# Masking the second batch's scores by bfloat16 factors on TensorE in a fused attention and Fourier-mixing kernel

## The chip, the cores and the metric

The kernel runs on one core of a Trainium2 chip. The metric is the time of one execution on the device in microseconds, of the slowest core; here there is only one core. Times are medians over several runs. A profile is one execution recorded by the hardware profiler, with its own time.

The engines are named as in the profile: PE is TensorE (matmuls; its weight loads are PEld), DVE is VectorE, ACT is ScalarE, POOL is GpSimd, and SP is SyncE, which here only issues DMAs. Every engine executes its own instructions in the order in which the program issued them.

## The reference

Four batches, eight heads, 768 positions, head dimension 64. Block-sparse attention with a mask of 32 x 32 blocks is followed by a Fourier mixing layer with two channel matmuls:

```python
scores = scale * np.matmul(q, k.transpose(0, 1, 3, 2))
# mask: neighbouring, first, last and sampled blocks; it is the same for all batches and heads
scores = np.where(mask, scores, -1000000000.0)
scores = scores - np.max(scores, axis=-1, keepdims=True)
attn = np.exp(scores)
attn = attn / (np.sum(attn, axis=-1, keepdims=True) + 1e-09)
x = np.matmul(attn, v)                      # then (B, H, S, D) -> (B, S, H*D)

X = np.fft.fft(np.fft.fft(x, axis=1), axis=2)
u = x + np.real(X)
un = (u - mean(u)) / np.sqrt(var(u) + 1e-06)
out = u + np.maximum(un @ w_ch1, 0.0) @ w_ch2
```

The mask depends on block rows and block columns alone, so the additive form of it is a product of two thin factors: one has a row per key block, the other says for every query which blocks are off.

## The kernel before

**Pairs, units and slots.** Heads are taken in pairs, and `n` counts the 16 pairs, four to a batch (`NP` = 4). The scores of a pair are computed with keys on the partitions: `half` chooses 384 of the 768 queries (`HS`), `c` chooses 128 of the keys, and one such piece for both heads is a unit `u`, twelve to a pair (`UP`). Two units make a slot (`SLOT`), so a pair has six slots, a batch has 24 (`SB`), and attention has 96. Batch 0 is slots 0 to 23, batch 1 is slots 24 to 47, and batch 2 begins at slot 48.

**One slot.** `slot(sl)` first issues `scores` for its two units: four logical matmuls (L551) into PSUM tiles `s`, of which there are two, one per unit. Then `weigh` makes the weights `e` of each unit (four buffers). Then `values` multiplies the `e` of the slot before with v into `o` (L597). After that come loads, transposes of the next pair's q and k (`turn`, L486), placing of results in x (`place`, L619), and steps of the mixer.

**How batch 0 is masked.** For `n < NP` the scores of both units are followed by two more matmuls a unit (L559). They add the product of the bfloat16 factors `of_k` and `off_q` to the same PSUM accumulation, so that masked scores become hugely negative. The exponential on ScalarE (L569) then writes `e` directly. The factors lie in two buffers with the tag `acc`. The sums over keys of this batch are made on TensorE (`add_up`, L663).

**How the later batches are masked.** For `n >= NP` the exponential is taken in place in PSUM (L572), and VectorE multiplies it with a table of zeros and ones in bytes into `e` (L574). GpSimd adds the `e` of a half up in `acc` (L584, two adds a unit from the second unit on), in the same two `acc` buffers that held the factors. `total` (L677) sums that over the partitions once a pair.

**The mixer and the channels.** When a batch's attention is done, `begin` appends its mixer's steps to the queue `apart`: division by the sums, folds on VectorE, cosine and sine matmuls (`along`, `across`), adding to x (`arrive`), normalisation (`spread`, `whiten`), transposes (`un_flip`, L917) and combinations for a Strassen-like product (`right`, `left`). The last entry of that queue has the kind "-"; it moves the list `rest` into `late`. `late` holds the channel matmuls (`quad`, L992, and `channels`, L1048), which are 155.6 us of planned TensorE time for a batch.

**What sets the order.** The order of the whole program is fixed when it is built. A planner keeps a modelled clock of each engine in `when`; `busy(engine, us, after)` advances one. `gap` takes steps from `apart` as long as the modelled clocks allow it: a VectorE step (kind "d" or "w") is taken when VectorE's clock would stay within a lead over TensorE's (3.0 us while no channels are waiting, 2.2 otherwise), and a TensorE step when its bank and the step before it are ready. Planned costs are written beside the steps: 0.72 us for the scores of a unit, 0.25 for its two mask matmuls, 0.75 for its values, 0.8 for its exponential, 0.97 for its mask multiplication, 2.0 for its two adds on GpSimd.

**When channels run.** Once channels wait in `late`, a slot takes between 2.5 and 9.6 us of them, so that about 100 us (`COVER`) are left for the start of the next batch. In slot 53 `until` runs whatever is left in `apart` and `late` until the first half of batch 0 is stored, because x has two buffers per half.

**Buffers and queues that the change touches.** `room(i, ...)` gives one of six large buffers. During batch 0 they hold raw weights: `w_load` brings chunk i to buffer i % 6, and `w_round` rounds it on ScalarE and VectorE; there are 32 chunks. The mixer uses buffers 0 and 1 for its folds, 4 and 5 for combinations, and the channels use 2 and 3 for hidden values. All the DMAs of this stretch but the first few are issued by SP, in the order of the program; in slot 21 these are the q loads of pair 5 (`load_q`, L252), which wait until pair 4's q has been read.

Of the kernel before, what the change touches and what calls it, by code (L numbers as in the profile page):

```python
# [12 lines left out]
BF16 = mybir.dt.bfloat16  # L13
# [4 lines left out]
ALU = mybir.AluOpType  # L18
ACT = mybir.ActivationFunctionType
# [83 lines left out]
def kernel(  # L103
# [14 lines left out]
    nc = tc.nc  # L118

    B, H, S, D = q.shape  # L120
    DM = H * D
    FF = w_ch1.shape[1]
    P = 128
    C = S // P
# [3 lines left out]
    HS = S // 2  # L128
# [7 lines left out]
    scale = 1.0 / float(D) ** 0.5  # L136
    KA = D + NB
    NP = H // 2
# [27 lines left out]
    mask = const.tile([P, C, S], U8, name="mask")  # L166
# [25 lines left out]
    def busy(engine, us, after=0.0):  # L192
        when[engine] = max(when[engine], after) + us
        return when[engine]
# [11 lines left out]
    HOP = 0.1  # L206
# [94 lines left out]
    def warm(n):  # L301

        m = ps_m.tile([P, P], FP32, tag="m", name="warm")
        for _ in range(n):
# [5 lines left out]
                         func=ACT.Exp)  # L310
# [124 lines left out]
    def room(i, shape, name, dtype=FP32):  # L435
        return big.tile(shape, dtype, tag=f"big{i}", name=name)
# [29 lines left out]

    turned, e_of, acc_of, o_of, sums_of, x_of, sp_of = {}, {}, {}, {}, {}, {}, {}
    s_at, e_at, oT_at, acc_at = {}, {}, {}, {}  # L470

# [64 lines left out]
    def scores(us):  # L536

        n, w = divmod(us[0], UP)
        half = w // C
        qT, kT = turned[n, 0], turned[n, 1]  # L540
        queries = slice(half * HS, (half + 1) * HS)
        got = []
        for u in us:
            c = u % C
            s = ps_s.tile([P, 2, 512], FP32, tag="s", name="s")
            got.append((u, s))
            busy("PE", 0.72, max(e_at.get(u - SLOT, 0.0), z_at[u % 2]))
            s_at[u] = when["PE"] + HOP
            for i in range(2):
                rows = slice(D * i, D * i + D)  # L550
                nc.tensor.matmul(s[:, i, 0:HS], kT[rows, c * P:(c + 1) * P], qT[rows, queries],  # L551
                                 start=True, stop=n >= NP)
        for u, s in got if n < NP else ():
            c = u % C
            busy("PE", 0.25)
            s_at[u] = when["PE"] + HOP
            for i in range(2):
                rows = slice(D * i, D * i + D)
                nc.tensor.matmul(s[:, i, 0:HS], of_k[rows, c * P:(c + 1) * P], off_q[rows, queries],  # L559
                                 start=False, stop=True)  # L560
        return got

    def weigh(u, s):
        n, w = divmod(u, UP)
        half, c = divmod(w, C)
        e = ep.tile([P, 2, HS], FP32, tag="e", name="e")
        e_of[u] = e
        if n < NP:
            nc.scalar.activation(out=e, in_=s[:, :, 0:HS], func=ACT.Exp, scale=scale)  # L569
            e_at[u] = busy("ACT", 0.8, s_at[u]) + HOP  # L570
            return
        nc.scalar.activation(out=s[:, :, 0:HS], in_=s[:, :, 0:HS], func=ACT.Exp, scale=scale)  # L572
        m = mask[:, c, half * HS:(half + 1) * HS].rearrange("p (o s) -> p o s", o=1)
        nc.vector.tensor_tensor(out=e, in0=s[:, :, 0:HS], in1=m.broadcast_to([P, 2, HS]),  # L574
                                op=ALU.mult)
        e_at[u] = busy("DVE", 0.97, busy("ACT", 0.8, s_at[u]) + HOP) + HOP
        if c > 0:
            acc_at[n, half] = busy("POOL", 2.0, e_at[u]) + HOP
        if c == 1:
            acc_of[n, half] = acc_p.tile([P, 2, HS], FP32, tag="acc", name="acc")  # L580

        for i in range(2 if c > 0 else 0):
            acc = acc_of[n, half][:, i, :]
            nc.gpsimd.tensor_add(out=acc, in0=e_of[u - 1][:, i, :] if c == 1 else acc,  # L584
                                 in1=e[:, i, :])
# [665 lines left out]
    def begin(b):  # L1251


        before, after, rest = mixer(b, x_of[b, 0], x_of[b, 1])
        any_of = len(late) + len(apart) + 4 * len(rest)
        hold = 2 * T
        apart.extend((*step, any_of) for step in norm_steps(b) + before)
        apart.extend((*step, hold) for step in after)
        apart.append(("-", lambda: late.extend(rest), 0.0, 0.0, 0.0, hold))

    def w_loads():
        while state["got"] < min(len(wchunks), state["w"] + ROOMS):
# [3 lines left out]
    def w_steps(sl):  # L1266
        while state["w"] < min(len(wchunks), W_PACE * sl):
            w_round(state["w"])
            state["w"] += 1

    def slot(sl):
        phase, r = divmod(sl, SB)
        n, s = divmod(sl, SP)
        units = range(SLOT * sl, SLOT * sl + SLOT)
        if sl < B * SB:
            for u, ps in scores(units):
                weigh(u, ps)
        if not late:
            gap(1.5)
        if 0 < sl <= B * SB:  # L1280
            done = [u - SLOT for u in units]
            for u in done:
                values(u)
            if phase == 0 or sl == SB:
                add_up(done)
            for u in done:
                e_of.pop(u)
        if s == 3 and n + 2 < len(pairs):
            load_q(n + 2)
        if s == 0 and 0 < n < len(pairs) - 1:  # L1290
            load_k(n + 1)

        reuse = n % NP == 0 and phase >= 2
        if sl > 0 and s == (5 if reuse else 3) and sl <= B * SB:
            b, j = pairs[n]
            at = oT_at[n, 0]
            if reuse:
                until(lambda: (b - 2, 0) in finished)
                at = when["PE"] + LEAVES
            if in_blocks(n):  # L1300
                place_blocks(n, 0)
            else:
                short.append(("t", at, lambda: place(n, 0)))
        if 0 < sl <= B * SB and s == 0 and n % NP != 1:
            if in_blocks(n - 1):
                place_blocks(n - 1, 1)
            else:
                short.append(("t", oT_at[n - 1, 1], lambda: place(n - 1, 1)))
        if sl < B * SB and n % NP == 1 and s == 1:
            b = pairs[n - 1][0]  # L1310
            at = oT_at[n - 1, 1]
            if b >= 2:
                until(lambda: (b - 2, 1) in finished)
                at = when["PE"] + LEAVES
            short.append(("t", at, lambda: place(n - 1, 1)))
        if sl > SB and s == 0 and sl <= B * SB:
            short.append(("t", acc_at[n - 1, 1], lambda: total(n - 1)))
        if n + 1 < len(pairs):
            for at, a, half in ((1, 0, 0), (2 if n > 0 else 3, 0, 1), (4, 1, 0), (5, 1, 1)):
                if s == at and n + 1 < BY_VECTOR:  # L1320
                    short.append(("t", 0.0, lambda a=a, half=half: turn(n + 1, a, half)))
            if s == 1:
                load_v(n + 1)
        if sl == 0:
            short.append(("t", 0.0, lambda: turn(0, 1, 1)))
        if sl == 1:
            short.append(("t", 0.0, lambda: turn(0, 0, 1)))
        if phase == 0 and 4 <= sl < 4 + 2 * C:
            short.append(("m", 0.0, lambda: mask_step(sl - 4)))
        if r == 1 and 0 < phase:  # L1330
            begin(phase - 1)
        left = SB * (phase + (0 if r == 0 else 1)) + 1 - sl
        us = sum(step[1] for step in late)
        pace = max(LEAST, min(MOST, (us - COVER) / left)) if left > 0 else MOST
        state["owed"] = min(state["owed"], pace) + pace if late else 0.0
        gap(max(state["owed"], 0.0))
        while late and state["owed"] >= late[0][1] / 2:
            state["owed"] -= late[0][1]
            channel_step()
            gap(max(state["owed"], 0.0))  # L1340

        while short and (s in (2, 5) or len(short) > 1 or phase == 0 or r == 0):
            ready = [i for i in short if max(i[1], min(free[i[0]])) <= when["PE"] + 0.1]
            if not ready and s not in (2, 5) and r > 0 and sl > 1:
                break
            item = ready[0] if ready else short[0]
            short.remove(item)
            item[2]()
        if BY_VECTOR <= n + 1 < len(pairs):
            for at, fn, args in ((0, squares, (n + 1, 0)), (1, flip_blocks, (n + 1, 0)),  # L1350
                                 (2, in_order, (n + 1,)), (4, flip_blocks, (n + 1, 1)),
                                 (5, squares, (n + 1, 1))):
                if s == at:
                    fn(*args)
        w_loads()
        w_steps(sl)
        if sl >= 4 and sl % 2 == 0:
            table_step()

# [139 lines left out]
```

## Time and profile before

| What | us |
|---|---|
| median of 9 runs | 1094.52 (1091.46 to 1095.35) |
| the profiled execution | 1093.16 |
| its span, first to last instruction | 1091.2 |
| busy in the span: PE | 1050.7 (96%) |
| DVE | 675.2 (62%) |
| ACT | 379.2 (35%) |
| POOL | 270.1 (25%) |
| mask multiplications L574, 144 of them | 131.1, 948 ns each |
| adds L584 on POOL, 192 and 48 | 196.7 and 49.6 |
| mask matmuls L559 of batch 0, 96 of them | 11.8 |

The page gives, for each group of instructions, its line, engine and operation, its tiles, how many there are, the busy time and the mean of one; behind a bar stands how long the engine was idle before them and what ended that. The mean of one contains overlap with its neighbours: a matmul of L559 lasts 323 ns by itself, but the 96 of them keep TensorE busy for 11.8 us.

The span in 40 equal slices of 27.3 us shows where the engines are full. A digit is the busy share in tenths, PEclk the clock that TensorE was granted:

```profile
PE   8999988988999999999999999999999999999996
DVE  5899878498754525564567535555556355575663
POOL 1000277688000001255546000244540001000000
PEclk9999999999999999999999999999999999999999
```

Slices 5 to 10 are batch 1 and the first slots of batch 2: TensorE is not full there, while VectorE and GpSimd are at their densest. From slice 11 on TensorE is full up to the last slice.

### The profile page before, as it was taken

Reading aid. Unit: us, or ns where it says so; the run is one execution under the profiler, and the core shown is the slowest. Engines: PE = TensorE matmul, PEld = TensorE weight load, DVE = VectorE, ACT = ScalarE, POOL = GpSimd, SP = SyncE. Lnnn points to the kernel's source line nnn. Section 1 sums busy time; section 2 is a strip of 40 time slices with the busy share of each in tenths; the row PEclk is TensorE's granted clock in tenths of the full one; section 3 lists DMA queues with packets and bytes.
Section 4 is the critical chain, followed back from the end, with each engine's and each line's share of the span. In section 5 each row is a group of like instructions: output and inputs, shape, how many; then the busy total and the mean of one; then the engine's idle time right before and its main releaser. Section 6 shows DMA issues by size and latency. Waiting matters only on the chain.

```text
span 1091.2 us, 12419 instructions
## 1 busy us (share of the span) xinstructions
PE 1050.7 (96%) x4334; PEld 535.6 (49%) x4334; DVE 675.2 (62%) x1241; ACT 379.2 (35%) x762; POOL 270.1 (25%) x302
## 2 busy tenths in 40 slices
PE   8999988988999999999999999999999999999996
PEld 4433333533555545443444545443344555568575
DVE  5899878498754525564567535555556355575663
ACT  5988655555111102353342202334230302220210
POOL 1000277688000001255546000244540001000000
PEclk9999999999999999999999999999999999999999
DMA  7757211021000000222211000221000001000001
GB/s 222 226 166 239 80 44 44 16 52 36 0 1 1 0 1 26 61 38 44 55 22 34 0 1 10 55 44 39 13 8 8 1 1 29 30 1 1 1 17 45
DMA packets 108194, 46.66 MB, mean 43 GB/s; under 512 B 95822, under 2 KB 100956, under 8 KB 108124
## 3 DMA queue, kind: packets, MB, share of 16 engines
q1 hardware_dynamic: 106236, 44.99, 16.3%
q10 hardware_dynamic: 1856, 0.79, 0.3%
q8 instruction: 36, 0.59, 0.2%
q14 instruction: 34, 0.28, 0.1%
q0 software_dynamic: 32, 0.01, 0.0%
HBM read 37.11 MB, written 6.29 MB: 40 GB/s over the span
## 4 chain that ended last, share of the span: by engine, by line
PE 83%; DVE 9%; ACT 2%; issue 2%; DMA 1%; POOL 1%; DVEq 0%; ACTq 0%; POOLq 0%
PE y L1048 23%; PE z L992 15%; PE s L551 10%; PE o L597 8%; PE yp L992 7%; PE yy L1111 6%; PE xp L992 3%; DVE e L574 3%; PE zp L805 2%; PE zp L776 1%; PE sp L663 1%; DMA out_dram<-x 1%; PE tp L486 1%; DVE x L855 1%; POOL acc L584 1%
## 5 line engine op out<-in xcount | busy, mean ns | idle before, releaser
L584 POOL TENSOR_TENSOR acc<-acc,e 128x384 f32<-128x384 f32 x192 | 196.7, 1058 | 84.3 <-DVE e L574 83.7
L551 PE MATMUL s<-qT,kT 64*128 64x384 f32 x768 | 158.0, 524 | 13.5 <-DVE e L574 11.8
L574 DVE TENSOR_TENSOR e<-s,mask 128x768 f32<-128x768 f32 x144 | 131.1, 948 | 58.9 <-ACT s L572 54.2
L572 ACT ACTIVATE s<-s 128x768 f32<-128x768 f32 x144 | 109.7, 791 | 112.8 <-PE s L551 111.7
L597 PE MATMUL o<-e,vr 128*64 128x384 f32 x768 | 146.7, 503 | 0.0
L1051 DVE TENSOR_TENSOR x<-y,x 128x512 f32<-128x512 f32 x72 | 49.7, 690 | 139.7 <-PE y L1048 139.6
L1048 PE MATMUL y<-w_sb,hA 128*128 128x512 f32 x288 | 129.8, 597 | 1.1 <-ACT zs L807 1.1
L1048 PE MATMUL y<-w_sb,hB 128*128 128x512 f32 x288 | 128.7, 597 | 1.0 <-DVE x L1051 1.0
L551 PEld LDWEIGHTS s<-qT,kT 64*128 64x128 f32 x768 | 63.8, 187 | 89.5 <-DVE e L574 41.9
L584 POOL TENSOR_TENSOR acc<-e 128x384 f32<-128x384 f32 x48 | 49.6, 1054 | 221.1 <-DVE e L574 171.8
L997 DVE TENSOR_TENSOR hA<-z,hA 128x384 f32<-128x384 f32 x64 | 35.7, 557 | 96.3 <-PE z L992 96.3
L992 PE MATMUL z<-unT,t 128*128 128x384 f32 x256 | 93.0, 486 | 0.0
L868 POOL TENSOR_SCALAR st<-st 128x1 f32<-128x1 f32 x24 | 6.6, 276 | 346.9 <-DVE st L867 346.5
L1048 PEld LDWEIGHTS y<-w_sb,hB 128*128 128x128 f32 x288 | 53.3, 190 | 68.5 <-issue 66.5
L597 PEld LDWEIGHTS o<-e,vr 128*64 128x64 f32 x768 | 47.0, 137 | 77.2 <-issue 71.7
L1048 PEld LDWEIGHTS y<-w_sb,hA 128*128 128x128 f32 x288 | 52.9, 190 | 64.8 <-issue 58.3
L1001 ACT ACTIVATE hA<-hA 128x384 f32<-128x384 f32 x64 | 33.4, 523 | 120.1 <-DVE hA L997 119.9
L992 PEld LDWEIGHTS z<-unT,t 128*128 128x128 f32 x256 | 48.6, 190 | 33.9
L1001 ACT ACTIVATE hB<-hB 128x384 f32<-128x384 f32 x64 | 33.5, 523 | 86.3 <-DVE hB L997 86.3
L992 PE MATMUL xp<-unT,w_sb 128*128 128x384 f32 x128 | 48.9, 505 | 1.3 <-DVE x L1051 0.7
L1012 ACT COPY hA<-xp 128x384 f32<-128x384 f32 x32 | 15.3, 478 | 100.0 <-PE xp L992 100.0
L992 PE MATMUL yp<-unT,w_sb 128*128 128x384 f32 x128 | 46.9, 489 | 0.4 <-DVE un L841 0.4
(200 smaller groups left out, 1390.0 us busy)
## 6 DMA issues: line engine op xcount, KB each, us to landing
wraw<-in_moe_w_ch_dram SPq DMA_DIRECT2D x32, 512.0 KB
vr<-in_v_dram SPq DMA_DIRECT2D x30, 192.0 KB
qr<-in_q_dram SPq DMA_DIRECT2D x48, 64.0 KB
x<-oT SPq DMA_DIRECT2D x192, 12.0 KB
kr<-in_k_dram SPq DMA_DIRECT2D x14, 192.0 KB
qb<-in_q_dram SPq DMA_DIRECT2D x28, 96.0 KB
kb<-in_k_dram SPq DMA_DIRECT2D x28, 96.0 KB
out_dram<-x SPq DMA_DIRECT2D x16, 128.0 KB
```

The source lines that it names most:

```text
L551: nc.tensor.matmul(s[:, i, 0:HS], kT[rows, c * P:(c + 1) * P], qT[rows, queries], start=True, stop=n >= NP)
L572: nc.scalar.activation(out=s[:, :, 0:HS], in_=s[:, :, 0:HS], func=ACT.Exp, scale=scale)
L574: nc.vector.tensor_tensor(out=e, in0=s[:, :, 0:HS], in1=m.broadcast_to([P, 2, HS]), op=ALU.mult)
L584: nc.gpsimd.tensor_add(out=acc, in0=e_of[u - 1][:, i, :] if c == 1 else acc, in1=e[:, i, :])
L597: nc.tensor.matmul(o[D * i:D * i + D, :], vt[:, i, c, :], e[:, i, :], start=(c == 0), stop=(c == C - 1))
L805: nc.tensor.matmul(ps[:, 0:KS - 1], sd[:, t, parts[g - 2]], sn_sb[:, t, :], start=(t == 0), stop=(t == T - 1))
L992: nc.tensor.matmul(to, a[:, k, :], c[:, k, :], start=(k == 0), stop=(k == ND // 2 - 1))
L997: tt(out=to, in0=ps, in1=a, op=ALU.add)
L1001: nc.scalar.activation(out=h, in_=h, func=ACT.Relu)
L1048: nc.tensor.matmul(y, hs[0, half][:, l, m * P:(m + 1) * P], w2_sb[:, 4 * r + l, :], start=(l == 0), stop=(l == 3))
L1051: nc.vector.tensor_tensor(out=x[:, m, :], in0=y, in1=x[:, m, :], op=ALU.add)
L1111: nc.tensor.matmul(ps, a[:, k, :], c[k // 2][:, k % 2, :] if isinstance(c, list) else c[:, k, :], start=(k == 0), stop=(k == 3))
```

## The change

In the slots after slot 21, until the step "-" of the first mixer is taken, the scores are masked as in batch 0: behind the score matmuls of both units come the bfloat16 mask matmuls, and the exponential writes `e` directly. From that step on, VectorE multiplies as before. The choice is made for each unit when `scores` is called, and the set `by_pe` remembers it for `weigh`. The condition does not name the batch: it asks whether the factors are still there.

Because the adds of batch 1 need the two `acc` buffers, the factors are copied at the end of slot 21 (`SB - 3`) into large buffer 2 by two DMAs on SP, 128 partitions of 1536 bytes each. From then on the mask matmuls read the copy, in slots 22 and 23 of batch 0 too. The step "-" sets `factors["at"]` to None beside moving the channels to `late`. The planner's costs follow: 0.25 us on TensorE for a unit masked there, and no 0.97 us on VectorE. GpSimd's adds and the sums of the batches are as before.

```diff
+    by_pe = set()
+    factors = {"at": (of_k, off_q)}
+
+    def keep_factors():
+
+        kept = room(2, [P, 2, S], "factors", BF16)
+        for a, t in enumerate(factors["at"]):
+            nc.sync.dma_start(out=kept[:, a, :], in_=t)
+        factors["at"] = kept[:, 0, :], kept[:, 1, :]
...
             got.append((u, s))
+            if n < NP or (factors["at"] and True):
+                by_pe.add(u)
...
-                                 start=True, stop=n >= NP)
-        for u, s in got if n < NP else ():
-            c = u % C
+                                 start=True, stop=u not in by_pe)
+        for u, s in got:
+            if u not in by_pe:
+                continue
+            c, (at_k, at_q) = u % C, factors["at"]
             busy("PE", 0.25)
...
-                nc.tensor.matmul(s[:, i, 0:HS], of_k[rows, c * P:(c + 1) * P], off_q[rows, queries],
+                nc.tensor.matmul(s[:, i, 0:HS], at_k[rows, c * P:(c + 1) * P], at_q[rows, queries],
                                  start=False, stop=True)
...
-        if n < NP:
+        if u in by_pe:
             nc.scalar.activation(out=e, in_=s[:, :, 0:HS], func=ACT.Exp, scale=scale)
             e_at[u] = busy("ACT", 0.8, s_at[u]) + HOP
+        else:
+            nc.scalar.activation(out=s[:, :, 0:HS], in_=s[:, :, 0:HS], func=ACT.Exp, scale=scale)
+            m = mask[:, c, half * HS:(half + 1) * HS].rearrange("p (o s) -> p o s", o=1)
+            nc.vector.tensor_tensor(out=e, in0=s[:, :, 0:HS], in1=m.broadcast_to([P, 2, HS]),
+                                    op=ALU.mult)
+            e_at[u] = busy("DVE", 0.97, busy("ACT", 0.8, s_at[u]) + HOP) + HOP
+        if n < NP:
             return
-        nc.scalar.activation(out=s[:, :, 0:HS], in_=s[:, :, 0:HS], func=ACT.Exp, scale=scale)
...
-        apart.append(("-", lambda: late.extend(rest), 0.0, 0.0, 0.0, hold))
+
+        def go():
+            late.extend(rest)
+            factors["at"] = None
+        apart.append(("-", go, 0.0, 0.0, 0.0, hold))
...
         w_steps(sl)
+        if sl == SB - 3:
+            keep_factors()
```

More of the change, by code (lines that the diff above doesn't have):

```diff
@@ L567, in weigh @@
         e_of[u] = e
-        if n < NP:
+        if u in by_pe:
             nc.scalar.activation(out=e, in_=s[:, :, 0:HS], func=ACT.Exp, scale=scale)
             e_at[u] = busy("ACT", 0.8, s_at[u]) + HOP
-            return
-        nc.scalar.activation(out=s[:, :, 0:HS], in_=s[:, :, 0:HS], func=ACT.Exp, scale=scale)
[L573 to L576, printed above, removed]
+        else:
[5 more added lines that the diff above has]
+        if n < NP:
+            return
         if c > 0:
```

## The prediction

> **What bounds the kernel now.** I read four views in this order: the busy table by stretch, the list of waits of TensorE in the second batch, the order in time around its first slot and around the DMA queue that the change uses, and the occupation of GpSimd.
>
> The busy table (columns: stretch, length, then busy time of PE, PEld, DVE, ACT, POOL, the granted clock, DMA share):
> ```profile
> 0.00:127.50 127.50, 121.64 (x802) 52.23 (x802) 106.64 (x251) 104.32 (x215) 3.68 (x14) 1.00 0.66 196
> 127.50:271.50 144.00, 126.47 (x672) 55.30 (x672) 109.17 (x150) 78.54 (x164) 108.70 (x111) 0.96 0.17 40
> 271.50:292.20 20.70, 20.09 (x61) 11.56 (x61) 16.28 (x31) 5.11 (x10) 2.75 (x2) 0.93 0.00 1
> 292.20:1091.20 799.00, 782.49 (x2804) 416.55 (x2802) 443.07 (x811) 191.27 (x374) 155.01 (x176) 1.00 0.09 20
> ```
> TensorE sets the time: 782 of the last 799 us are busy, and of the 16.5 us missing there about nine are the last stretch's output. The one place with slack is 127.5 to 271.5, the second batch and the first slots of the third: 17.5 us idle, and a clock below 1.
>
> Who ends that idle time, and how:
> ```profile
> PE s L551 <- DVE e L574: 9.8, 8, 2.5
> PE utp L917 <- DVE un L880: 3.1, 1, 3.1
> PE tp L486 <- ACT qT L495: 2.2, 2, 1.1
> ```
> ```profile
> 126.96 0.55 PE L619 MATMUL xt<-ident,oT 128*128 128x128 f32 x3
> 129.78 2.22 PE L551 MATMUL s<-qT,kT 64*128 64x384 f32 x8 [2.27 <-DVE e L574]
> ```
> The scores of a unit need one of two pairs of banks, which the mask multiplication on VectorE releases; VectorE is in order and has weight rounding or the mixer's folds ahead of it. After the stall matmuls run slower: the eight L597 from 131.92 took 2.72 us, against 1.51 elsewhere.
>
> I priced the loss by full-speed spacing. Scores start 1.49 us before their values (150.21 to 151.70), values take 1.44 (to 153.15): 2.93 us a slot. From 127.43 to 271.45 TensorE has 29 slots (85.0), 16 groups of k and x transposes at 0.47-0.48 (7.6), four q turns at 0.95 (3.8), four sums of 0.78, the mixer's along and across steps (9.15 and 4.8), six flips (3.5), two inversions (0.9): 117.9 of 144.0, so 26.1 lost. The two quads that follow end at 292.16 and lose 2.3 more. **Lost: 28.4 us**, by place 4 around 128, 5 up to 150, 6.6 from 150 to 185, 5.6 to 244, 1.9 to 266, 5.7 to 292.
>
> **What the skill says.** (1) "TensorE: Matmul & The Clock Gate", part 1: the clock halves after an idle window of about 3.4 us. The trace agrees in kind, though stalls of 2.3 and 2.5 us already brought it. (2) "SBUF — State Buffer", "Who interferes with whom": a VectorE operation with two SBUF inputs and a GpSimd one that reads SBUF exclude each other for a whole instruction; one with a single SBUF input doesn't contend outside the two-port modes. The trace fits: next to adds, a two-element copy (L740) took 0.96 us, and the similar L857 at 242.10 took 0.15. The mask multiplication has one SBUF input, so its removal frees no port, but it takes away VectorE time in which GpSimd ran undisturbed. (3) "DMA: Bandwidth & Descriptors", "Anatomy of one DMA": about 2.0 us fixed plus bytes over 436 GB/s, fitted on GpSimd's queue. The one landing that this trace has, 13.5 KB on that queue, took 3.0 us; for SP's queue no run here shows it.
>
> **The change, part by part.**
>
> *Copy of the factors.* Two DMAs of 128 x 1536 B at the end of slot 21 go behind q's load on SP:
> ```profile
> 109.45 0.38 SPq L440 DMA_DIRECT2D wraw<-in_moe_w_ch_dram  x1
> 110.67 3.82 SPq L252 DMA_DIRECT2D qr<-in_q_dram  x6
> ```
> SP is free at 114.49. The buffer is free: its last rounded chunk, the 27th, ends at 110.75. Behind both SP has nothing until 124.69, so they delay no load. Landing, an estimate by (3): 114.5 + 0.4 for the second issue + 2.0 + 0.39 MB / 436 GB/s (0.9) = 117.8. But slot 22 already reads the copy: its mask matmuls stand at 115.13. TensorE is in order, so values, x and k transposes of the slot wait too: 2.7 us (1.5 to 6), with the slower clock behind it 1.3 (0 to 2). New loss: 4.
>
> *The masks.* In batch 0 a slot's scores to its values take 1.82 us (109.21 to 111.03) with four bfloat16 matmuls; without, 1.49. So 0.33 us per slot of two units is added. It lasts until the planner takes the step that starts the channels; there is no test for the batch, so it lasts into the third if that comes late. In the kernel before, the start came only at 271, forced in slot 53. The chain of steps up to it has planned costs of 40.9 us VectorE, 18.7 TensorE, 8.4 ScalarE, one after the other, some 68; each of its 18 TensorE steps also waits for the next gap, of which there are two a slot, about 1.2 us: 90. A planned slot costs 3.44 us (0.72+0.25+0.75 twice) and some 0.6 of transposes; with masks no longer on VectorE, nothing else holds the chain. 4.05 N + 18.7 = 90 to 98 gives N = 18 to 20; I take slots 24 to 43, **20 slots: 6.6 us added** (16 to 30 slots: 5.3 to 9.9).
>
> *What leaves.* 40 multiplications of 0.948 us on VectorE, 38 us: on the path only through the waits above. The exponential writes e itself, 0.82 for 0.79 us on ScalarE, which has room (78.5 of 144).
>
> *What is late next.* Around 128, the 4 us before disappear and the 4 of the copy take their place: no gain. To 150: clock and waits on e go, the waits of a q turn on ScalarE (1.1 each) stay: 2.5 of 5. From 150 to 185 the folds run while GpSimd is already full: 4.84, 5.00, 5.00 and 4.84 of 5 us in
> ```profile
> 160.00:165.00 5.00, 4.83 (x5) 1.00 0.04 14
> 165.00:170.00 5.00, 5.00 (x5) 1.00 0.02 5
> 170.00:175.00 5.00, 5.00 (x5) 1.00 0.35 79
> 175.00:180.00 5.00, 4.84 (x5) 1.00 0.00 0
> ```
> Its 20 adds per pair of heads need 20 us alone (1.00 each), and TensorE's pair then takes 6 x 3.26 + 3.6 = 23.2. Folds and scalings ask some 12 us of the same port within seven slots; 23 adds more make 35 against TensorE's 29. Four e tiles allow about one slot of lag, so ScalarE, then TensorE, wait for the rest: 3.5 of 6.6 remain. From the along steps to slot 43: flips behind slow VectorE steps, 3 of 5.6. The later slots have channels to fill waits, 1.5 of 1.9; the start of the channels is no longer forced at one place, 0.5 of 5.7. Sum of the new losses 4 + 2.5 + 3.5 + 3 + 1.5 + 0.5 = 15.
>
> *Moved.* Some 55 us of channels go from one block behind slot 53 into slots 43 to 48 (the pace is capped at 9.6 per slot). TensorE's work is the same wherever it stands; there the masks are on VectorE again, 1.9 + 5.6 us a slot against 13 of TensorE. Slot 53 still forces batch 0 to its end in both kernels, and 88 us remain as cover for the next mixer, whose first steps took 280 to 366. So nothing after it changes.
>
> **Sum.** 28.8 by places (28.4 by count) lost before, 15 after, 6.6 added: 7.2 us less. The profiled execution took 1093.16 (span 1091.2 and 1.96 around it): 1086.0. It stands 1.36 below the median of the runs, so 1087.3.
>
> **Rivals.**
> *A, the forecast*: 1083 to 1092, chance 0.46.
> *B, the waits go almost entirely*: the port holds nobody and the copy lands early; losses 8, result 1080. For it: batch 0 with the same matmuls has PE busy 121.6 of 127.5, first loads included. Against: the queue order above. 0.16.
> *C, the channels start no sooner*: 30 slots cost 9.9, the forced 5.7 stays, a loss of about 19: 28.8 - 19 - 9.9 = 0: 1094.5. For it: real VectorE steps are longer than planned (folds and scalings 20.8 against 15). Against: the planner goes by its own costs. 0.1.
> *D, slower: GpSimd's adds become the bound.* Without masks VectorE sends two-input operations back to back, and each add waits for one. From slot 24 to 36 there are 40 adds and 51 us of TensorE; at 1.15 to 1.25 us, as contended adds took, they fit. From 1.45 they need 58, 7 us over, which cancels the gain; at 1.55, 62, 11 over: 1098. For it: the four rows above. Against: the folds end, and adds beside along steps are free. A copy landing 5 us later would do the same. 0.28.
>
> The chances of faster, same and slower count 0.2% (2.2 us), about what a measurement of this kernel can tell from no change: faster 0.61 (A, B less 0.01), same 0.11, slower 0.28. The likeliest case alone has 1083 to 1092; with B and the near part of D the range is 1079 to 1098.
>
> **What would show it.** A wait of TensorE on a DMA of the copy in slot 22 near 115 us, 2 to 4 us long; none on VectorE's e from slot 24; four bfloat16 matmuls a slot until around slot 43, and the first product of a quad well before the third batch. D shows as ScalarE's exponential waiting for GpSimd, and adds above 1.4 us. The forecast is wrong if the copy costs over 6 us or if idle time between slots 24 and 43 stays above 15.

## The result, and the profile after

| | before | changed |
|---|---|---|
| median of the runs, us | 1093.82 (1091.46 to 1095.35, 30 runs) | 1087.94 (1084.66 to 1090.86, 10 runs) |
| ratio, 95% interval | 1 | 0.9949 (0.9939 to 0.9959) |
| span of the profiled execution, us | 1091.2 | 1086.1 |

The kernel is faster by 5.9 us in the medians and by 5.1 us in the profiles. Single runs of the changed kernel lie up to 6.2 us apart, so its profile shows one of several possible courses. The channels now start at 227 us, in slot 42, instead of at 271 in slot 53. So TensorE masks 19 slots of batch 1, slots 24 to 42. Line numbers have moved: scores are L565, mask matmuls L575, values L615, mask multiplications L590, GpSimd's adds L602, the first cosine step L794 to L796.

First, who ended idle time of TensorE in the second batch of the changed kernel, over 107 to 300 us (columns: total us, times, longest). Tiles of the program stand in front: `s` is scores, `zp` a cosine step, `tp` a transpose, and `sa` and the `e` of L767 are folds:

```profile
PE s L575 <- DMA factors<-at_q: 3.8, 1, 3.8
PE zp L794 <- DVE sa L767: 3.7, 1, 3.7
PE tp L498 <- ACT qT L507: 2.2, 2, 1.1
PE zp L795 <- DVE e L767: 0.7, 1, 0.7
PE s L565 <- ACT e L585: 0.3, 1, 0.3
```

The waits on VectorE's e, 9.8 us before, are gone, and so is the forced flip at 270. Two waits are new: on the copy of the factors, and on VectorE's folds.

Second, the busy table by stretch, for the changed kernel (columns as before). The first three rows run from the scores of slot 22 to 330 us; the next runs on to the scores of slot 58, from where both kernels issue the same work; the last is the rest:

```profile
113.21:160.00 46.79, 38.24 (x231) 16.36 (x232) 37.16 (x57) 25.88 (x50) 25.11 (x19) 0.96 0.19 49
160.00:227.00 67.00, 65.17 (x403) 32.49 (x401) 32.74 (x61) 38.05 (x84) 47.15 (x54) 1.00 0.14 36
227.00:330.00 103.00, 102.69 (x390) 48.02 (x387) 57.83 (x87) 35.78 (x71) 36.84 (x36) 1.00 0.10 20
330.00:462.15 132.15, 129.68 (x441) 67.05 (x439) 75.78 (x148) 31.62 (x67) 22.09 (x27) 1.00 0.08 19
462.15:1086.10 623.95, 608.62 (x2241) 326.42 (x2241) 351.40 (x631) 154.19 (x295) 139.28 (x154) 0.99 0.10 21
```

The same two parts of the kernel before, from slot 22 to slot 58 and the rest:

```profile
113.68:469.41 355.73, 336.25 (x1383) 162.87 (x1384) 230.54 (x388) 132.16 (x272) 126.49 (x134) 0.98 0.11 25
469.41:1091.20 621.79, 606.61 (x2243) 326.09 (x2241) 351.21 (x631) 154.07 (x295) 139.97 (x155) 1.00 0.10 21
```

From slot 22 to slot 58 the changed kernel takes 348.94 us instead of 355.73: 6.8 less. Its four rows have 13.2 us of idle TensorE, against 19.5. TensorE's busy time is nearly equal although 6.3 us of mask matmuls came in: time at the slow clock and score groups split by a wait (1.78 us instead of 1.56) went out, together some 7 us, an estimate from the durations of the matmuls in both traces. VectorE is busy for 27 us less. Two thirds of the idle time that is left, 8.6 us of 13.2, lie in the first row, which is also the only one of the four with a granted clock below 1. The last part then gives 2.2 us back, although it does the same work.

### The profile page after: what moved, and what is told of

Same layout as the page of the kernel before. It is cut to its first block, busy times and chain, and to the rows that moved or that the text cites. A ratio compares the mean times of both kernels' runs of the same rounds, so it can differ in the third digit from the quotient of the medians.

```text
span 1086.1 us, 12509 instructions
## 1 busy us (share of the span) xinstructions
PE 1051.8 (97%) x4410; PEld 536.7 (49%) x4410; DVE 648.3 (60%) x1203; ACT 378.6 (35%) x762; POOL 274.2 (25%) x302
## 4 chain that ended last, share of the span: by engine, by line
PE 89%; DVE 5%; ACT 2%; DMA 2%; issue 1%; SPq 1%; DVEq 0%; ACTq 0%
PE y L1066 23%; PE z L1010 15%; PE s L565 11%; PE o L615 11%; PE yp L1010 8%; PE yy L1129 6%; PE xp L1010 4%; PE zp L823 2%; PE sp L681 1%; PE tp L498 1%; PE utp L935 1%; PE s L575 1%; PE sp L695 1%; PE zp L794 1%; PE xt L637 1%
## 5 line engine op out<-in xcount | busy, mean ns | idle before, releaser
L602 POOL TENSOR_TENSOR acc<-acc,e 128x384 f32<-128x384 f32 x192 | 200.4, 1077 | 128.5 <-DVE e L590 119.1
L565 PE MATMUL s<-qT,kT 64*128 64x384 f32 x768 | 154.2, 517 | 5.2 <-DVE e L590 3.8
L615 PE MATMUL o<-e,vr 128*64 128x384 f32 x768 | 147.0, 504 | 0.0
L590 DVE TENSOR_TENSOR e<-s,mask 128x768 f32<-128x768 f32 x106 | 96.3, 948 | 46.8 <-ACT s L588 45.1
L588 ACT ACTIVATE s<-s 128x768 f32<-128x768 f32 x106 | 80.2, 789 | 118.3 <-PE s L565 112.7
L602 POOL TENSOR_TENSOR acc<-e 128x384 f32<-128x384 f32 x48 | 49.9, 1060 | 233.8 <-ACT e L585 128.4
L565 PEld LDWEIGHTS s<-qT,kT 64*128 64x128 f32 x768 | 63.7, 186 | 80.1 <-issue 23.0
L615 PEld LDWEIGHTS o<-e,vr 128*64 128x64 f32 x768 | 47.0, 137 | 75.3 <-issue 71.2
L585 ACT ACTIVATE e<-s 128x768 f32<-128x768 f32 x86 | 65.1, 813 | 28.0 <-PE s L575 26.6
```

Of the source, the lines that this page charges most:

```text
L615: nc.tensor.matmul(o[D * i:D * i + D, :], vt[:, i, c, :], e[:, i, :], start=(c == 0), stop=(c == C - 1))
```

## The experiments

Each is compared with the kernel before. Experiments 1 to 4 and 6 test steps of the forecast, 5 tries to use what they showed, and 7 and 8 follow from its miss. The kernel before was measured again beside each group, with medians from 1093.82 to 1094.63, and each ratio is taken within its group. The intervals are 1 to 2 us to either side, so a difference of that size between two experiments decides nothing by itself. Where an edit adds or takes lines, the line numbers shift by up to three.

| | us | ratio, 95% interval |
|---|---|---|
| changed kernel | 1087.94 | 0.9949 (0.9939 to 0.9959) |
| 1: batch 0 reads the originals | 1082.53 | 0.9895 (0.9879 to 0.9910) |
| 2: masks on TensorE, old order | 1091.61 | 0.9979 (0.9969 to 0.9989) |
| 3: new order, masks on VectorE | 1095.67 | 1.0019 (1.0010 to 1.0028) |
| 4: few adds on GpSimd | 1080.98 | 0.9893 (0.9875 to 0.9911) |
| 5: 1, with measured folds | 1098.21 | 1.0035 (1.0021 to 1.0049) |
| 6: 1, with masks twice | 1086.58 | 0.9938 (0.9924 to 0.9951) |
| 7: 1, values before the cosine step | 1084.42 | 0.9912 (0.9899 to 0.9926) |
| 8: 1, cosine step one slot later | 1108.27 | 1.0130 (1.0114 to 1.0145) |

### 1. What the copy costs

The order in time of TensorE around slot 22 in the changed kernel:

```profile
113.21 1.61 PE L565 MATMUL s<-qT,kT 64*128 64x384 f32 x8 [0.34 <-ACT e L585]
118.60 0.50 PE L575 MATMUL s<-factors 64*128 64x384 bf16 x4 [3.77 <-DMA factors<-at_q]
119.03 0.55 PE L637 MATMUL xt<-ident,oT 128*128 128x128 f32 x3
119.51 2.47 PE L615 MATMUL o<-e,vr 128*64 128x384 f32 x8
121.91 1.51 PE L681 MATMUL sp<-e,pick 128*32 128x384 f32 x8
```

and its DMA queue:

```profile
114.14 0.56 SPq L478 DMA_DIRECT2D factors<-at_k  x1
114.74 0.60 SPq L478 DMA_DIRECT2D factors<-at_q  x1
```

The mask matmuls of slot 22 stand still for 3.77 us until 3.9 us after the second DMA was issued, and the matmuls behind them run slow: 2.47 us for values that take 1.51, 1.51 for sums that take 0.85. Slots 22 and 23 belong to batch 0, though, and the originals are still there. The edit:

```diff
-            c, (at_k, at_q) = u % C, factors["at"]
+            c, (at_k, at_q) = u % C, factors["at"] if n >= NP else (of_k, off_q)
```

> Slots 22 and 23 of batch 0 read the factors where they were made; only batch 1 reads the copy, which is still made at the end of slot 21. Theory: the wait for the copy (3.8 us) and the slower matmuls behind it (1.6 us: the eight value matmuls took 2.47 instead of 1.51, the sums 1.51 instead of 0.85) were lost in full, so the time falls by 4.5 to 5.5 us against the changed kernel, to 0.990 of the kernel before (0.9885 to 0.991). Rival: the wait let VectorE finish its weight rounding, and comes back at the first cosine step, which then waits about 9 us for VectorE instead of 4.4: the time stays within 1.5 us of the changed kernel, ratio 0.994 to 0.996.

The time is 5.4 us below the changed kernel. The copy is issued at the same place (113.83 and 114.43), slot 22 runs through, and its values take 1.51 us:

```profile
114.39 0.49 PE L575 MATMUL s<-at_q,at_k 64*128 64x384 bf16 x4
115.29 1.51 PE L615 MATMUL o<-e,vr 128*64 128x384 f32 x8
```

The wait for the folds does not grow: 3.65 us in that profile. So the copy cost its whole wait and the slow clock behind it, within what the medians can tell, and nobody else used the pause. This is the fastest version of the study that does the whole computation, 11.8 us below the kernel before.

### 2 and 3. The masks without the order, the order without the masks

The change does two things: it moves work from VectorE, and it tells the planner so, which then starts the channels eleven slots sooner. Experiment 2 keeps the planner's old costs:

```diff
-            busy("PE", 0.25)
-            s_at[u] = when["PE"] + HOP
+            if n < NP:
+                busy("PE", 0.25)
+                s_at[u] = when["PE"] + HOP
...
             e_at[u] = busy("ACT", 0.8, s_at[u]) + HOP
+            if n >= NP:
+                e_at[u] = busy("DVE", 0.97, e_at[u]) + HOP
```

> The masks are made by TensorE as in the changed kernel, but the planner counts 0.97 us on VectorE and nothing on TensorE for them, so every step stands where it stood in the kernel before; the channels start in slot 53 and 30 slots are masked by TensorE. Theory (the order brings about half of the gain, the waits on the weights e the rest): waits of TensorE on VectorE's e vanish, the forced start at the channels (5.7 us) stays, 30 x 0.33 = 9.9 us are added: 1089 to 1094, ratio 0.996 to 1.0. Rival (the waits on e are the whole gain, the order nothing): 1087 to 1089, ratio 0.993 to 0.9955.

1091.6 us, inside what the theory said. The profiled execution took 1088.9, a fast one among its 21 runs. Of the waits on VectorE's e in this stretch none is left, but the forced start of the channels stays. Who ended TensorE's idle time, 107 to 300 us, experiment 2:

```profile
PE s L576 <- DMA factors<-at_q: 3.4, 1, 3.4
PE tp L498 <- ACT qT L507: 2.7, 3, 1.1
PE z L1013 <- DVE t L975: 2.3, 1, 2.3
PE utp L938 <- DVE un L901: 1.9, 1, 1.9
```

The third and fourth lines are that start. So without its order, and with 30 slots masked by TensorE instead of 19, the change is worth 2.7 us instead of 5.9. The masks of eleven more slots, an estimated 3.6 us at 0.33 each, are as large as that whole difference: the earlier start pays at least in part by ending the masks sooner.

Experiment 3 keeps the new order and leaves the masks of batch 1 on VectorE, with neither copy nor mask matmuls there:

```diff
...
-                                 start=True, stop=u not in by_pe)
+                                 start=True, stop=n >= NP)
...
-            for i in range(2):
+            for i in range(2 if n < NP else 0):
...
-        if u in by_pe:
+        if n < NP:
...
-            e_at[u] = busy("DVE", 0.97, busy("ACT", 0.8, s_at[u]) + HOP) + HOP
+            e_at[u] = busy("ACT", 0.8, s_at[u]) + HOP
+            if u not in by_pe:
+                e_at[u] = busy("DVE", 0.97, e_at[u]) + HOP
```

> The converse: the order of the changed kernel, with channels from slot 43 on, but the masks of batch 1 are multiplied on VectorE as before; no copy of the factors and no mask matmuls in batch 1. It saves 6.3 us of TensorE and the 5.4 us of the copy against the changed kernel. Theory (VectorE is what held the stretch): VectorE has some 36 us of masks besides 55 us of mixer steps before the channels begin, TensorE waits on e and on the folds: 1088 to 1096, ratio 0.995 to 1.002, with 12 us or more of waits on VectorE in the second batch. Rival (the order alone brings it, and VectorE has room): 1076 to 1083, ratio 0.984 to 0.990.

1095.7 us, within the theory's interval, though the 6.3 us of mask matmuls (19 slots at 0.33) and the 5.4 us of the copy are gone from it. Its waits on VectorE, 107 to 300 us, come to 11.8 us, a little under the 12 that were expected; the two largest:

```profile
PE s L562 <- DVE e L587: 7.9, 5, 3.0
PE xt L636 <- DVE sums L664: 3.2, 1, 3.2
```

Each half alone brings less than the whole, or nothing: the early order gains only where VectorE is free of the masks.

### 4. Why the first cosine step waits

The order of VectorE in the changed kernel, from the reciprocal before the scalings (L723) through the folds:

```profile
139.68 0.45 DVE L718 RECIPROCAL r<-r 128x48 f32<-128x48 f32 x1
140.17 6.24 DVE L723 TENSOR_TENSOR x<-x,r 128x512 f32<-128x512 f32 x6
146.44 2.44 DVE L746 TENSOR_TENSOR sa<-x 128x1536 f32<-128x1536 f32 x1
148.80 2.56 DVE L746 TENSOR_TENSOR sd<-x 128x1536 f32<-128x1536 f32 x1
...
157.85 1.34 DVE L767 TENSOR_TENSOR sa<-sa 128x384 f32<-128x384 f32 x1
159.23 1.24 DVE L768 TENSOR_TENSOR sa<-sa 128x384 f32<-128x384 f32 x1
160.39 1.08 DVE L767 TENSOR_TENSOR e<-e 128x128 f32<-128x128 f32 x1
```

and of GpSimd, in which each line merges adds that follow each other:

```profile
135.63 9.03 POOL L602 TENSOR_TENSOR acc<-acc,e 128x384 f32<-128x384 f32 x8 [1.91 <-ACT e L585]
145.88 3.86 POOL L602 TENSOR_TENSOR acc<-e 128x384 f32<-128x384 f32 x2 [1.22 <-ACT e L585]
149.70 11.62 POOL L602 TENSOR_TENSOR acc<-acc,e 128x384 f32<-128x384 f32 x8
```

Both engines are slow together: eight adds in 11.62 us are 1.45 us each, against 1.00 alone, and VectorE has no idle time from 140.17 on. Experiment 4 leaves adds out, so that the sums of batch 1 no longer run over all keys:

```diff
-        for i in range(2 if c > 0 else 0):
+        for i in range(2 if c > 0 and (c == 1 or n >= 2 * NP) else 0):
```

> The changed kernel with GpSimd's adds of batch 1 left out from the third unit of a half on (8 of 10 adds; the sums of batch 1 are then over two units only). Theory: the wait of the first cosine step on VectorE's folds (3.65 + 0.71 us) comes from GpSimd's adds holding the port that scalings and folds need; without them the folds take about 15 us instead of 21 and the wait goes: 4 to 5 us less than the changed kernel, ratio 0.990 to 0.9915. Rival: the folds take as long alone, the planner's costs are simply too low: the wait stays above 3 us, ratio 0.994 to 0.9955.

It is 7.0 us below the changed kernel, more than expected, and the wait for the folds is gone. The same operations of VectorE in experiment 4:

```profile
138.63 0.45 DVE L718 RECIPROCAL r<-r 128x48 f32<-128x48 f32 x1
139.12 3.70 DVE L723 TENSOR_TENSOR x<-x,r 128x512 f32<-128x512 f32 x6
142.85 1.76 DVE L746 TENSOR_TENSOR sa<-x 128x1536 f32<-128x1536 f32 x1
...
150.47 0.55 DVE L767 TENSOR_TENSOR sa<-sa 128x384 f32<-128x384 f32 x1
151.06 0.56 DVE L768 TENSOR_TENSOR sa<-sa 128x384 f32<-128x384 f32 x1
151.54 0.28 DVE L767 TENSOR_TENSOR e<-e 128x128 f32<-128x128 f32 x1
```

The six scalings take 3.70 instead of 6.24 us, and a fold of 128 elements 0.28 instead of 1.08. From the first scaling to the last step that the cosine waits for, VectorE needs 13.0 us instead of 21.6. (In the profiles, some 1.6 us of the gain are a slow clock in slot 82 that the changed kernel's execution had, see below.) The reciprocal has one SBUF input and takes 0.45 us with and without adds beside it. So it is GpSimd's adds beside VectorE's operations with two SBUF inputs that make the wait, as the Trainium skill's "SBUF — State Buffer", "Who interferes with whom", describes: the second input and GpSimd's reads share one port.

### 5, 7 and 8. Trying to cover that wait

If the planner underprices the folds, telling it the truth should put other work in front of the cosine step. Experiment 5, on top of experiment 1, also sets a scaling of batch 0 to 1.05:

```diff
...
-        first = [d(1.8, fold_0, 0), d(1.8, fold_0, 1), d(1.0, fold_1, 0), d(0.9, fold_e),
-                 d(1.0, fold_1, 1), d(1.2, fold_2, 0), d(0.6, fold_2, 2), d(1.3, fold_2, 1)]
+        took = (2.4, 2.5, 1.7, 3.2, 1.7, 2.5, 1.4, 1.2) if b == 0 else (1.8, 1.8, 1.0, 0.9, 1.0, 1.2, 0.6, 1.3)
+        first = [d(us, *f) for us, f in zip(took, ((fold_0, 0), (fold_0, 1), (fold_1, 0), (fold_e,), (fold_1, 1), (fold_2, 0), (fold_2, 2), (fold_2, 1)))]
```

> As the first experiment (batch 0 reads the original factors), and the planner is told for batch 0's scalings and folds what they took in the profile of the changed kernel (1.05 us a scaling instead of 0.9; folds 2.4, 2.5, 1.7, 3.2, 1.7, 2.5, 1.4, 1.2 instead of 1.8, 1.8, 1.0, 0.9, 1.0, 1.2, 0.6, 1.3). Theory: the planner then takes the first cosine step one or two slots later, scores and values stand in front of it, and its wait of 3.6 us goes; one or two more slots are masked by TensorE (0.33 each): 2.5 to 4 us less than the first experiment, ratio 0.986 to 0.9875. Rival: the wait only moves to another step of the chain, or the channels start so much later that it is lost again: ratio 0.989 to 0.991.

Both theory and rival fell: 1098.2 us, 15.7 above experiment 1. The wait for the folds did go, but a different one stood in its place, and later ones appeared. Places from the order of TensorE in experiment 5:

```profile
156.72 1.78 PE L695 MATMUL sp<-acc,pick 128*32 128x384 f32 x4 [1.99 <-POOL acc L602]
...
297.92 2.57 PE L565 MATMUL s<-qT,kT 64*128 64x384 f32 x8 [3.64 <-DVE e L590]
```

The first is the sum over a pair, which now meets GpSimd's adds before they are done. In the second, the scores of slot 51 wait for masks that stand behind three scalings of batch 1 and a transpose on VectorE; the nearest such wait of experiment 1, in slot 50, is 0.30 us. The channels start in slot 45 instead of 42, and with them the order of everything after.

Experiments 7 and 8 look for the least shift that covers the wait. Experiment 7 puts the values of slot 30 before the cosine step. The order of VectorE stays the same, and that of TensorE changes in slots 30 to 35:

```diff
...
-        if not late:
+        if not late and sl != 30:
             gap(1.5)
```

> As the first experiment, but in slot 30 the planner's look for mixer steps between scores and values is left out: the first cosine step then comes behind the values of slot 30 (1.44 us of TensorE that wait for nothing), and the order of VectorE stays exactly the same. Theory (the wait for the folds is a wait in TensorE's queue alone): the wait falls from 3.6 to about 2.2 us and the time by 1.4: ratio 0.9885 (0.987 to 0.9895). Rival (what comes later is set by something else, as in the fifth experiment): no gain, ratio 0.9895 to 0.992.

There is no gain, as the rival said: 1084.4 us, 1.9 above experiment 1, with intervals that overlap. The wait itself fell as the theory computed, from 3.65 to 2.20 us, but a wait of 0.7 us of a q transpose on ScalarE is new. At slot 58 experiment 7 is 0.13 us behind experiment 1 in the two profiles, having begun slot 22 0.69 behind it: about half a microsecond is gained. Then the same 1.7 us wait on VectorE stands at slot 58 in both. Behind it the clock differs; experiment 7:

```profile
457.11 1.79 PE L565 MATMUL s<-qT,kT 64*128 64x384 f32 x8 [1.72 <-DVE e L590]
458.83 2.83 PE L615 MATMUL o<-e,vr 128*64 128x384 f32 x8
```

and experiment 1:

```profile
456.98 1.78 PE L565 MATMUL s<-qT,kT 64*128 64x384 f32 x8 [1.73 <-DVE e L590]
458.69 1.51 PE L615 MATMUL o<-e,vr 128*64 128x384 f32 x8
```

Experiment 8 lets no cosine step be taken in slot 30:

```diff
...
-            if len(late) > need:
+            if len(late) > need or (at_slot[0] == 30 and kind == "m"):
                 break
...
+        at_slot[0] = sl
```

> As the first experiment, but the planner may not take the first cosine step in slot 30, so that it comes in slot 31; later mixer steps and the start of the channels move by about one slot, and one more slot is masked by TensorE. Theory (the loss of the fifth experiment, some 16 us, came from its channels starting three slots later, behind slots whose scores wait for VectorE): the wait of 3.6 us goes, and about a third of that loss, 5 us, comes in: ratio 0.9895 to 0.993. Rival (the later start costs only its masks, 0.33 us; the fifth experiment lost by one unlucky place): the whole wait is gained, 1079 to 1080, ratio 0.986 to 0.988.

1108.3 us, far outside both. The wait for GpSimd's sums came again (2.30 us), and the moved order met a new one in the last batch, here in the order of TensorE and of ScalarE:

```profile
717.68 0.48 ACT L638 COPY x<-xt 128x384 f32<-128x384 f32 x1 [10.02 <-DMA out_dram<-x]
...
718.22 1.12 PE L935 MATMUL utp<-ident,un 128*128 128x128 f32 x4 [7.29 <-ACT x L638]
```

A result of batch 3 is to be copied into the buffer of x whose output of batch 1 is still being stored. ScalarE waits for that DMA, and TensorE 7.29 us for the bank that ScalarE should empty. So a shift of one slot at 150 us decides over a wait at 710. The starts of slots 22, 58 and 95 in the profiles divide the losses against experiment 1 by stretch. Of experiment 8's 25.8 us, 10.0 arise between slots 22 and 58, 6.2 from there to slot 95, and 8.8 behind it. Experiment 5, 15.2 us behind in the profiles, had begun slot 22 2.7 us later; it loses 7.6 us, gains 1.0, and loses 5.9 in the same three stretches. Which waits make up these sums was not separated.

### 6. The price of a mask matmul

```diff
-                nc.tensor.matmul(s[:, i, 0:HS], at_k[rows, c * P:(c + 1) * P], at_q[rows, queries],
-                                 start=False, stop=True)
+                for again in range(2 if n >= NP else 1):
+                    nc.tensor.matmul(s[:, i, 0:HS], at_k[rows, c * P:(c + 1) * P], at_q[rows, queries],
+                                     start=False, stop=again == (1 if n >= NP else 0))
```

> As the first experiment, with the mask matmuls of batch 1 issued twice; the planner is told nothing, so the order stays. Theory: each mask matmul lies on the path of TensorE, at 0.33 to 0.43 us a slot in 19 slots, 6.3 to 8.2 us, of which some 1.5 us in the four slots between the inversion and the first cosine step fall into its wait for VectorE: 4.5 to 7 us more than the first experiment, ratio 0.9935 to 0.996. Rival: TensorE has enough small gaps in these slots to hide them: less than 2.5 us more, ratio up to 0.992.

4.05 us more than experiment 1: the path carries the masks, a little less of them than expected. The profiles say why. Between slots 31 and 43, experiment 6 falls behind by 0.32 us with every slot (from 0.48 to 4.32 us over 12 slots). In the slots from 24 to 30 it falls behind too, by 1.9 us in all, but then its first cosine step waits that much less for VectorE. So the masks of the first seven slots cost next to nothing in these two kernels; those of the other twelve cost their full time.

## Why the prediction was right

The forecast was 1087.3 us and the measurement 1087.94; it gave 7.2 us of gain where the medians show 5.9. That the two times lie closer than the two gains has a plain reason: the forecast started from the median of 9 runs, 1094.52, and the 30 runs have 1093.82. The direction and the mechanism were right (the waits on e go, and the copy, the folds and the masks take part of the gain back); the sizes of the single losses were not, and that their sum fits is in part luck. Step by step:

- **The masks.** 20 slots at 0.33, 6.6 us; it was 19 slots. A slot's scores to its values still take 1.82 us where nothing else stands between, 128.34 to 130.16, so 6.3. The planner's chain was counted right, from its own costs. Experiment 6 refines it: of a second set of masks, those of twelve slots were on the path, and those of the first seven fell into the wait for the folds.
- **The copy.** Expected 2.7 us of wait and 1.3 of slow clock; it was 3.77 and 1.6 (0.96 in the values and 0.66 in the sums), together 5.4 instead of 4. The landing estimate from "DMA: Bandwidth & Descriptors", "Anatomy of one DMA", 2.9 us, fell short: the mask matmuls started 3.9 us after the second issue began. Experiment 1 confirms the sum.
- **To 150 us.** Expected 2.5 left; one wait of 1.12 on a q turn remained, without a slow clock.
- **The folds.** 3.5 left, through the port shared with GpSimd; it was 4.36 (3.65 + 0.71), and experiment 4 confirms the port. But the way was not the forecast's: it expected ScalarE to wait for e tiles and TensorE behind it. No such wait appeared there; TensorE waited for the folds themselves, in the cosine step. Of the forecast's evidence, one piece was loose: the two-element copy has one SBUF input, not two. It was held all the same: 0.96 us beside adds in the changed kernel, 0.15 after them in experiment 4. The exception that the forecast named, the two-port modes, may be the reason, but no run shows the mode of that copy.
- **From the along steps to slot 43.** Expected 3, by flips behind slow VectorE steps; the flips ran free, and one q turn took 1.12.
- **The start of the channels and on to slot 58.** Expected 2 together; it was 2.8: one wait of 1.73 on e in slot 58, and three of 0.6 or less.
- **Sum.** Losses 14.8 where 15 were forecast: 1.4, 0.9 and 0.8 too little at the copy, the folds and the later slots, 1.4 and 1.9 too much up to 150 us and at the flips. The errors cancel. 28.8 - 14.8 - 6.3 is 7.7; the profiles show 6.8 up to slot 58. Part of the rest is in the moved channels: eight of their matmuls take 3.43 us in a row, and 3.53 when scores follow (252.55 to 256.08). That TensorE's work is the same wherever it stands was a little too simple.
- **Nothing after it changes.** That step was wrong by 2.2 us. From slot 58 the same work runs, but of a wait of 1.73 us in slot 82, which both kernels have, the changed kernel came out with the slow clock, which accounts for 1.6 us. The changed kernel, then the kernel before:

```profile
716.30 2.48 PE L565 MATMUL s<-qT,kT 64*128 64x384 f32 x8 [1.73 <-DVE e L590]
718.71 2.46 PE L615 MATMUL o<-e,vr 128*64 128x384 f32 x8
```
```profile
723.14 1.78 PE L551 MATMUL s<-qT,kT 64*128 64x384 f32 x8 [1.73 <-DVE e L574]
724.85 1.51 PE L597 MATMUL o<-e,vr 128*64 128x384 f32 x8
```

  Experiment 4, with the same order, shows no such slowing; experiment 1 has it. Only one execution of each kernel was traced, so how often it happens is not known.
- **The rivals.** B, 1080, asked for the copy to land early and the port to hold nobody; experiments 1 and 4 each take one of these away, and reach 1082.5 and 1081.0. C did not happen: the channels came early, and experiment 2 shows what it would have been with the old order, 1091.6, where C had 1094.5. D did not happen either: it needed a mean of 1.45 us over 40 adds. The ten beside the folds took 1.54 each, but the first 40 of batch 1 kept GpSimd busy for 46.55 us, 1.16 each, within the 1.15 to 1.25 with which the forecast let them fit.

## What to carry to other kernels

When an engine that is full in one stage is relieved, its loss can return in three forms that a profile of before already lets one price: the transfer that the new path needs first, the shared port that the relieved engine now uses without pause, and the engine that takes the work. In a program whose order a planner fixes, removing load changes the order too. Here the two belong together: the masks without the new order brought 2.7 of 5.9 us, the new order without the masks nothing. But repairing one visible wait through the planner moved waits elsewhere and lost up to 26 us against the same kernel without the repair, so a wait is better removed at its data (the first experiment, one expression, 5.4 us) than by shifting what stands around it. A copy made to free a buffer should be read only from the moment the original is needed for something else.

## What the runs showed of the hardware

- The same stall can be followed by slow matmuls or not. Twenty times in the ten traces, scores waited 1.72 to 1.74 us; five times the sixteen matmuls from there took 4.47 to 4.80 us, fifteen times 3.15. The eight value matmuls behind it took 2.83 us in experiment 7 and 1.51 in experiment 1, in programs whose order differs only in slots 30 to 35. Longer stalls show the same: four cosine matmuls behind 3.65 us took 1.56 us in the changed kernel and 2.93 in experiment 1. What decides was not shown; some 1.5 us of a result hang on it, and that limits what a comparison of two such kernels says.
- Two SBUF-to-SBUF DMAs of 128 rows of 1536 bytes on SP's queue were in use by TensorE 3.4 to 3.9 us after the issue of the second began, in experiments 2 and 4 and the changed kernel.
- Beside GpSimd's adds, VectorE's operations with two SBUF inputs took 1.04 instead of 0.62 us (scalings), 1.34 instead of 0.55 (folds of 384 elements) and 1.08 instead of 0.28 (folds of 128). Both of these folds lose 0.8 us, close to the 1.00 of an add alone, so the shorter the operation, the larger the factor.
